# Folded maximum scans for five head pairs, with 64 more scans moved into the front part

## The chip, the cores and the metric

The kernel runs on one core of one Trainium2 chip. The metric is the device time of one execution in microseconds (us). Three runs of the kernel before gave 1754.66, 1750.93 and 1756.15 us; their median is 1754.66 us.

## The reference

Two mixers of the same input x (2048 rows of 512 numbers, fp32) are blended row by row by a gate:

```python
qkv = x @ wqkv                                  # 32 heads of 16 numbers
scores = einsum("bhqd,bhkd->bhqk", q, k) * Dh ** -0.5
a = softmax(scores) @ v, heads joined, @ wo     # attention
b = Cr @ (x @ Wr.T) - Ci @ (x @ Wi.T)           # real part of a 2-D Fourier transform
g = sigmoid((x * gate_w).sum(-1))
out = g * a + (1 - g) * b
```

The weights of the attention are scaled by 64, so the scores are large and the softmax needs the true maximum of every row of scores: exp(score - max) is what is summed.

## The kernel before, in words

TensorE (PE) does all products as fp32r matmuls with 512 columns. A product of full precision is made of three partial products, high times high, high times low and low times high; the low part is the rest that the high part leaves. A contraction of 128 rows is cut into two halves of 64 rows that run side by side in the array (`halves_of`, L141). Such a side-by-side pair is called a slot here.

**Scan.** The maximum of every row of scores is found first, in a pass of its own, the scan. Two heads make a pair, and there are 16 pairs (`NP`). For one pair, `scan(n, ps)` (L110) takes a block of 128 queries (`qb`, 16 of them) and a quarter of the keys (`c`, 4 quarters of 512). It issues two matmuls side by side, one for each head (L119), into a PSUM tile of two banks, and VectorE (DVE) reduces the tile to two maxima for each of the 128 queries with one `tensor_reduce` (L121). So a pair has 64 scans (`SCANS`), and all pairs have 1024 (`TOTAL`). After the 64th, `shift(p)` (L123) takes the maximum over the four quarters, transposes, splits and stores it in DRAM (`m_d`); the attention later reads it as two more rows of the query operand, so that its scores arrive in PSUM with the maximum subtracted.

**Front part (L150 to L504).** Here PE makes the projections of x to q and k (`project_t`, L280), to values and to the hidden Fourier transform (`project_s`, L303), and then the Fourier transform along the sequence (L455 to L502). q and k go to DRAM as high and low part (`q_d`, `k_d`); `row_loads` (L76) brings back the rows of one pair, and in the front part these loads are issued on ScalarE's (ACT) queue (`load_scan_beside`, L175). `products` (L201) and the Fourier loop call `beside()` (L183) after every slot. It runs the helpers that are due (`after`, `run_due`), and once `PACE` (3.9) slots have passed it puts one scan into PE's order. A scan's PSUM tile is one of two (`s1`, L155), used in turn; the projections use the two others (`xy`). The front part issues the first `FRONT` (564) scans. Order on every engine is the order in which the code issues; nothing is reordered.

**Attention part (L506 to L780).** 512 steps, 32 for each pair: 2 halves of the queries (`h`) by 16 blocks of keys (`kb`). A step computes scores with `qk2` (L532) for two query chunks: chunk 0 into one tile of two banks that exists once (tag `s3`, `bank2`), chunk 1 into two single banks out of three (tag `s2`, `bank`). ACT takes the exponential of chunk 0 in one instruction (L547) and of chunk 1 in two (L551). `pv` (L556) multiplies the exponentials with the values; its 16 PE instructions per two steps accumulate into `pvb`. While scans are left (`next_scan`, L728), each step also holds one scan between the two `qk2` calls, and each step runs the `pv` of the step before.

From step `MIX` on (L38, 512 less the steps without a scan, so step 461) there are no scans. Then a generator, `outputs()` (L693), mixes the finished heads with wo: `next(fill)` (L755, L765) yields a few slots per step. `mix_heads(t, steps)` (L653) makes 9 slots for row block t, spread as `steps` says, and `take_in` (L644) adds the gated result to the Fourier part `ys[t]` on DVE. From `MIX` on the `pv` work is grouped: none in an odd step, that of two steps in an even one (L769). Before, `mix_heads` used 4 or 2 steps for a row block, in all 51 steps. The Fourier part is read back from `y_d` for the row blocks 0 to 7 eleven steps ahead of `MIX` and for the others at step 480 (L751, `load_y`). What is left after the last step (L783 to L827) is a tail of some output blocks.

Of the kernel before, what the change touches and what calls it, by code (L numbers as in the profile page):

```python
# [34 lines left out]
FRONT = 564  # L35
PACE = 3.9
NWARM = 20
MIX = TOTAL - FRONT + 1  # L38
SLOW = 3


def build(tc, x, xT, wqkv, wo, wrT, wiT, cr, ci, gate, out):
    nc = tc.nc
    with ExitStack() as ctx:
# [6 lines left out]
        k_d = [dram.tile([P, 2, S], F32, name=f"k_d{f}") for f in range(ND)]  # L51
        m_d = [dram.tile([2, 4, 2, NB, 32], F32, name=f"m_d{p}") for p in range(NP)]
# [23 lines left out]
        def row_loads(p, queue):  # L76
# [4 lines left out]
            for j in range(2):  # L81
                b, r = 64 * j, slice(DH * ((2 * p + j) % 8), DH * ((2 * p + j) % 8) + DH)
                loads += [(ks[b:b + 32, :], k_d[p // 4][r, 0:1, :].to_broadcast([DH, 2, S])),
                          (qs[b:b + 32, :], q_d[p // 4][r, :, :].rearrange("e n s -> (e n) s")),
                          (ks[b + 32:b + 48, :], k_d[p // 4][r, 1, :]),
# [22 lines left out]
        mx = {}  # L108

        def scan(n, ps):  # L110

# [9 lines left out]
            nc.vector.tensor_reduce(mx[p][:, :, qb, c], ps, axis=AX.X, op=ALU.max)  # L121

        def shift(p):  # L123
# [10 lines left out]
            return [lambda: nc.vector.tensor_reduce(m, mx[p].rearrange("p j b c -> p (j b) c"), axis=AX.X, op=ALU.max,  # L134
                                                    negate=True),
# [12 lines left out]
        seen, slots, due = [0], [0], []  # L148
        pace = [None, 0.0]
        with ExitStack() as pf:  # L150
# [11 lines left out]
            def after(n, f, *args):  # L162

                due.append((slots[0] + n, len(due), f, args))
# [18 lines left out]
            def beside():  # L183
# [5 lines left out]
                pace[1] += 1.0 / pace[0]  # L189
# [60 lines left out]
            with ExitStack() as px:  # L250
# [28 lines left out]

                def project_t(w, dst, f, c, ps=None):  # L280
# [4 lines left out]
                    s = ep.tile([P, 512], F32, tag="ty", name="s")  # L285
# [9 lines left out]
                    def store(i, v):  # L295
                        nc.sync.dma_start(dst[f][:, i, c * 512:(c + 1) * 512], v.bitcast(F32))

                    after(9, nc.scalar.copy, hi, s)
# [62 lines left out]
                project_t(wk, k_d, 1, 0)  # L361
# [72 lines left out]
            with ExitStack() as py:  # L434
# [4 lines left out]

                for n in range(4, 8):  # L440
# [63 lines left out]
        assert seen[0] == FRONT  # L504

        with ExitStack() as pa:  # L506
# [347 lines left out]
```

## Time and profile before

| what | value |
|---|---|
| median of three runs | 1754.66 us (1750.93 to 1756.15) |
| profiled execution | 1756.16 us |
| its span, first to last instruction | 1754.4 us |
| PE busy | 1731.9 us, 99% of the span |
| DVE busy | 1347.4 us, 77% |
| ACT busy | 1166.8 us, 67% |
| POOL busy | 777.5 us, 44% |
| scans (L121) | 1024 of 1220 ns each by the mean, 1208.4 us |
| mean granted PE clock | 0.998 |

How to read it: matmuls are pipelined and their ends are modelled, so that PE is shown busy in nearly the whole span whatever bounds it. What bounds a stage is read from the pitch, the time from one start to the next, and from what an instruction waited for. The profile gives a share of each engine in 40 slices of 43.9 us. DVE is full in the slices 3 to 16 (the front part), ACT is full from slice 18 on (the attention part) up to the last three slices, which hold the steps without a scan.

### The profile page before, as it was taken

The page shows a single profiled execution, that of the slowest core. Times are in us where ns is not written, and L with a number is a line of the kernel's source. Part 1 is how long each engine was busy: PE and PEld are TensorE (multiplying, and loading weights), DVE is VectorE, ACT ScalarE, POOL GpSimd, SP SyncE. Part 2 cuts the span into 40 slices and gives each one's busy share as a digit, 9 for nine tenths or more (in the row PEclk, how much of TensorE's full clock was granted, in tenths as well). Part 3 has the DMA queues.
Part 4 walks back from the last instruction along what each step waited for, and adds up shares of the span by engine and source line. Part 5 has one row for each costly group of instructions (what it writes and reads, how often), then busy time and mean ns, then how long its engine had stood idle before and what let it go on. Part 6 is the DMA issues. An engine that isn't in the chain of part 4 may idle for free.

```text
span 1754.4 us, 33571 instructions
## 1 busy us (share of the span) xinstructions
PE 1731.9 (99%) x13640; PEld 988.3 (56%) x13640; DVE 1347.4 (77%) x1296; ACT 1166.8 (67%) x1894; POOL 777.5 (44%) x881
## 2 busy tenths in 40 slices
PE   8999999999999999999999999999999999999998
PEld 6987787878777787633333333333333333333554
DVE  6799999999999999866666666666666777765233
ACT  6445333000031000299999999999999999999885
POOL 3688557666677777413232322323232323323222
PEclk9999999999999999999999999999999999999999
DMA  7662455525474553633233351441433333453512
GB/s 263 224 199 74 128 156 177 138 92 133 129 188 134 136 150 112 145 61 62 58 63 61 57 99 25 87 72 42 79 66 61 65 67 72 85 108 91 138 41 100
DMA packets 119307, 185.79 MB, mean 106 GB/s; under 512 B 53184, under 2 KB 55728, under 8 KB 112240
## 3 DMA queue, kind: packets, MB, share of 16 engines
q1 hardware_dynamic: 77200, 148.96, 32.7%
q0 software_dynamic: 38496, 19.47, 5.3%
q10 hardware_dynamic: 3456, 15.21, 4.1%
q8 instruction: 107, 1.75, 0.5%
q14 instruction: 48, 0.39, 0.1%
HBM read 129.89 MB, written 53.22 MB: 104 GB/s over the span
## 4 chain that ended last, share of the span: by engine, by line
PE 80%; DVE 12%; DMA 3%; POOL 2%; issue 1%; ACT 1%; SPq 0%; DVEq 0%; ACTq 0%; POOLq 0%
PE pvb L558 27%; PE xy L145 21%; PE s L543 18%; PE s L119 11%; DVE mx L121 11%; PE s L145 3%; DMA lc<-ob 2%; POOL s L173 1%; POOL el L173 0%; DVE b L214 0%; DMA q_d<-eh 0%; DMA raws<-xT 0%; DMA raws<-wqkv 0%; POOL lc L566 0%; DVE y L645 0%
## 5 line engine op out<-in xcount | busy, mean ns | idle before, releaser
L121 DVE TENSOR_REDUCE mx<-s 128x2 f32<-128x1024 f32 x1024 | 1208.4, 1220 | 276.2 <-PE s L119 276.1
L551 ACT ACTIVATE e<-s 128x512 f32<-128x512 f32 x1024 | 630.4, 748 | 1.6 <-PE s L543 1.6
L547 ACT ACTIVATE eb<-s 128x1024 f32<-128x1024 f32 x512 | 600.2, 1172 | 23.0 <-PE s L543 23.0
L558 PE MATMUL pvb<-e,va 128*17 128x512 f32 x2048 | 528.5, 599 | 0.0
L558 PE MATMUL pvb<-eb,va 128*17 128x512 f32 x2048 | 528.3, 599 | 0.0
L543 PE MATMUL s<-qs,ks 50*128 50x512 f32 x2048 | 454.1, 442 | 0.0
L543 PEld LDWEIGHTS s<-qs,ks 50*128 50x128 f32 x2048 | 215.3, 184 | 418.4 <-ACT eb L547 389.5
L119 PE MATMUL s<-ks,qs 48*128 48x512 f32 x2048 | 418.7, 397 | 8.4 <-DVE mx L121 6.9
L496 ACT ACTIVATE tx<-xy,gm 128x512 f32<-128x512 f32 x32 | 22.1, 689 | 380.6 <-PE xy L145 329.7
L119 PEld LDWEIGHTS s<-ks,qs 48*128 48x128 f32 x2048 | 200.3, 184 | 45.5 <-DVE mx L121 20.0
L566 POOL DMA_DIRECT2D lc<-ob x124 | 63.1, 515 | 238.9 <-DVE ob L563 238.8
L558 PEld LDWEIGHTS pvb<-eb,va 128*17 128x17 f32 x2048 | 63.4, 95 | 174.9 <-issue 163.7
L573 POOL DMA_DIRECT2D r_d<-lc x31 | 18.1, 585 | 322.3 <-DVE lc L572 322.3
L145 PE MATMUL xy<-w,b 64*128 64x512 f32 x768 | 105.4, 392 | 0.2 <-ACT s L292 0.2
L645 DVE SCALAR_TENSOR_TENSOR y<-s,g,y 128x512 f32<-128x512 f32 x50 | 36.6, 748 | 81.5 <-PE s L145 80.9
L310 ACT ACTIVATE tx<-xy 128x512 f32<-128x512 f32 x48 | 28.7, 598 | 93.1 <-PE xy L145 91.5
L575 POOL DMA_DIRECT2D rb<-r_d x124 | 60.3, 493 | 54.0 <-DMA r_d<-lc 53.9
L145 PEld LDWEIGHTS xy<-w,b 64*128 64x128 f32 x768 | 72.9, 186 | 17.0 <-ACT s L292 0.7
L576 POOL TENSOR_TENSOR ob<-ob,rb 128x512 f32<-128x512 f32 x31 | 39.7, 1282 | 70.6 <-DMA rb<-r_d 68.8
L408 POOL TENSOR_TENSOR ab<-tx,ty 128x512 f32<-128x512 f32 x32 | 41.3, 1291 | 50.6 <-ACT ty L311 32.2
L558 PEld LDWEIGHTS pvb<-e,va 128*17 128x17 f32 x2048 | 63.3, 95 | 0.3 <-ACT e L551 0.3
L173 POOL TENSOR_TENSOR el<-s,eh 128x512 fp32r<-128x512 f32 x32 | 41.4, 1295 | 48.2 <-ACT eh L173 41.0
(928 smaller groups left out, 2085.8 us busy)
## 6 DMA issues: line engine op xcount, KB each, us to landing
craw<-ci SPq DMA_DIRECT2D x64, 256.0 KB
craw<-cr SPq DMA_DIRECT2D x60, 256.0 KB
ks<-k_d SPq DMA_DIRECT2D x48, 256.0 KB
qs<-q_d SPq DMA_DIRECT2D x48, 256.0 KB
ab_d<-ab SPq DMA_DIRECT2D x32, 256.0 KB
y_d<-y SPq DMA_DIRECT2D x32, 256.0 KB
o_d<-oh POOLq DMA_DIRECT2D x28, 256.0 KB, 9.8
o_d<-ol POOLq DMA_DIRECT2D x28, 256.0 KB, 15.3
```

The source lines that it names most:

```text
L119: nc.tensor.matmul(ps[:, j, :], qs[b:b + 48, qb * P:(qb + 1) * P], ks[b:b + 48, c * 512:(c + 1) * 512], start=True, stop=True)
L121: nc.vector.tensor_reduce(mx[p][:, :, qb, c], ps, axis=AX.X, op=ALU.max)
L145: nc.tensor.matmul(ps[j], lhs[r], rhs[r], start=first, stop=last)
L173: d[2](*d[3])
L408: nc.gpsimd.tensor_add(ab, tx, ty)
L543: nc.tensor.matmul(pss[j], ks[b:b + 50, kb * P:(kb + 1) * P], qs[b:b + 50, q0:q0 + 512], start=True, stop=True)
L547: nc.scalar.activation(e, ps, AF.Exp, scale=SCALE)
L551: nc.scalar.activation(e[j], pss[j], AF.Exp, scale=SCALE)
L558: nc.tensor.matmul(pvb[r:r + VC, :], va[:, kb, 2 * p + j, :], es[c][j], start=kb == 0, stop=kb == NB - 1, tile_position=(0, r))
L566: nc.gpsimd.dma_start(lc[32 * n:32 * n + 32, :], ob[r + DH:r + VC, :].rearrange("p (s e) -> p s e", e=16))
L575: nc.gpsimd.dma_start(rb[r:r + DH, :], r_d[p][h][n:n + 1, :].to_broadcast([DH, 512]))
L576: nc.gpsimd.tensor_mul(ob, ob, rb)
```

## The change

For the pairs 4 to 8 (`FOLDED`) the keys of the four quarters are combined two by two. With a and b the keys of two neighbouring quarters, max(q.a, q.b) = relu(q.(a - b)) + q.b for each pair of keys. `kf_d` holds a - b in the place of the even quarters and b in the place of the odd ones; it is built while the keys are projected (`fold_keys`). A scan of an even quarter then ends in ACT, which writes the positive part of the 128x1024 PSUM tile to SBUF (`fold`). A scan of an odd quarter ends in two `tensor_tensor_reduce` on DVE, one for each head, which add the PSUM half and the `fold` half and give the maximum. PE's scans stay as many as before, 64 for a pair. These five pairs' 320 scans are issued at a closer pace, and `FRONT` is 628 instead of 564. So the attention part holds 396 scans, `MIX` is step 397, and 115 steps have no scan; the 9 slots of a `mix_heads` are spread over 6 or 8 steps. For the row blocks 8 to 12 `mix_heads` starts before `load_y`, so it loads its own rows of `y_d`; the blocks 8 to 11 are also stored back there. While k is projected the pace is 4.2. In the order of the built program each `tensor_tensor_reduce` is two DVE instructions, the pass itself and one that writes 128x1.

```diff
-FRONT = 564
+FRONT = 628
 PACE = 3.9
+FOLDED = range(4, 9)
+FOLD_PACE = 3.15
+SLOW_PACE = 4.2
-SLOW = 3
...
-            nc.vector.tensor_reduce(mx[p][:, :, qb, c], ps, axis=AX.X, op=ALU.max)
+            if p not in FOLDED:
+                nc.vector.tensor_reduce(mx[p][:, :, qb, c], ps, axis=AX.X, op=ALU.max)
+            elif c % 2 == 0:
+                fold[0] = folds[0].tile([P, 2, 512], F32, tag="fold", name="fold")
+                nc.scalar.activation(fold[0], ps, AF.Relu)
+            else:
+                for j in range(2):
+                    nc.vector.tensor_tensor_reduce(out=fold[0][:, j, :], in0=ps[:, j, :], in1=fold[0][:, j, :],
+                                                   scale=1.0, scalar=-3.0e38, op0=ALU.add, op1=ALU.max,
+                                                   accum_out=mx[p][:, j, qb, c // 2:c // 2 + 1])
...
-                scanned[p], loads = row_loads(p, nc.scalar if p else nc.sync)
+                scanned[p], loads = row_loads(p, nc.scalar if p else nc.sync, kf_d if p in FOLDED else k_d)
...
-                pace[1] += 1.0 / pace[0]
+                pace[1] += (PACE / FOLD_PACE if seen[0] // SCANS in FOLDED else 1.0) / pace[0]
...
+                def fold_keys(f, c):
+
+                    a, b = half.pop(c - 1), half.pop(c)
+                    hi = ep.tile([P, 512], F32R, tag="eh", name="eh", bufs=3)
+                    lo = ep.tile([P, 512], F32R, tag="el", name="el")
+                    nc.gpsimd.tensor_sub(a, a, b)
+
+                    def store(i, v):
+                        nc.sync.dma_start(kf_d[f][:, i, (c - 1) * 512:c * 512], v.bitcast(F32))
+
+                    after(4, nc.scalar.copy, hi, a)
+                    after(5, nc.vector.tensor_sub, lo, a, hi.bitcast(F32))
+                    after(8, store, 0, hi)
+                    after(12, store, 1, lo)
...
-                for n, (f, c) in enumerate([(2, 0), (3, 0)] + [(f, c) for f in range(1, ND) for c in range(1, NC)]):
-                    if n == 2:
+                for n, (f, c) in enumerate([(f, c) for f in range(1, ND) for c in range(NC)]):
+                    if n == 0:
+                        scan_at(SLOW_PACE)
+                    if n == 3:
                         load_w(wv, wqkv[:, 1024:1536], 48, nc.gpsimd)
                     project_t(wk, k_d, f, c)
+                scan_at(PACE)
...
                 ps = pair_banks()
+                if t not in ys:
+                    y = ap.tile([P, D], F32, tag="take", name="yb", bufs=3)
+                    nc.sync.dma_start(y, y_d[t // 4][:, t % 4, :])
...
+                alone = t not in ys
+                if alone:
+                    ys[t] = y
                 for j in range(2):
                     take_in(t, ps[:, j, :])
+                if alone:
+                    nc.sync.dma_start(y_d[t // 4][:, t % 4, :], ys.pop(t))
...
-                        yield from mix_heads(t, (2, 2, 2, 3) if t < 2 * SLOW and t % 2 == 0 else (4, 5))
+                        yield from mix_heads(t, (1, 1, 1, 1, 1, 1, 1, 2) if t in (0, 5, 10) else (1, 2, 1, 2, 1, 2))
```

More of the change, by code (lines that the diff above doesn't have):

```diff
@@ L51, in build @@
         k_d = [dram.tile([P, 2, S], F32, name=f"k_d{f}") for f in range(ND)]
+        kf_d = [None] + [dram.tile([P, 2, S], F32, name=f"kf_d{f}") for f in range(1, ND)]
         m_d = [dram.tile([2, 4, 2, NB, 32], F32, name=f"m_d{p}") for p in range(NP)]
@@ L74, in build, with row_loads @@
         scanned, used = {}, {}
-        def row_loads(p, queue):
+        def row_loads(p, queue, keys=k_d):
             qs = stk.tile([P, S], F32R, tag="stk", name="qs")
@@ L296, in store @@
                         nc.sync.dma_start(dst[f][:, i, c * 512:(c + 1) * 512], v.bitcast(F32))
+                        if folded and c % 2:
+                            nc.sync.dma_start(kf_d[f][:, i, c * 512:(c + 1) * 512], v.bitcast(F32))
+                    if folded:
+                        half[c] = s
+                        if c % 2:
+                            after(11, fold_keys, f, c)
                     after(9, nc.scalar.copy, hi, s)
```

23 lines of the change are left out of this document (13 added, 10 removed).

## The prediction

> **What bounds the kernel now.** I read the page's busy times first, then the busy times of three stretches, then the chain that ended last, and then the timeline of a few microseconds in each stage.
>
> ```profile
> PE 1731.9 (99%) x13640; PEld 988.3 (56%) x13640; DVE 1347.4 (77%) x1296; ACT 1166.8 (67%) x1894; POOL 777.5 (44%) x881
> ```
>
> PE is shown busy everywhere, so the line decides nothing. The stretches do (columns: PE, PEld, DVE, ACT, POOL busy, with the number of instructions):
>
> ```profile
> 361.00:737.00 376.00, 372.69 (x3176) 297.30 (x3172) 369.69 (x341) 43.37 (x70) 255.61 (x251) 1.00 0.51 137
> 1493.00:1613.40 120.40, 119.48 (x884) 43.70 (x880) 81.63 (x77) 119.62 (x191) 35.62 (x55) 1.00 0.44 95
> 1613.40:1735.50 122.10, 122.10 (x992) 63.83 (x993) 36.66 (x53) 101.24 (x154) 26.17 (x39) 1.00 0.33 86
> ```
>
> The first stretch is the front part from the first scan of pair 4 (the first one to be folded) to its end. DVE is full (370 of 376 us) and ACT nearly idle (43), so DVE looks like the limit, and folding moves work from DVE to ACT. But PE is full too. The chain shows its pitch:
>
> ```profile
> 36.79 20.02 PE xy L145 x173
> 1631.31 1.84 PE pvb L558 x16
> 1635.68 1.84 PE pvb L558 x16
> 1640.73 1.84 PE pvb L558 x16
> 1728.16 1.84 PE pvb L558 x16
> 1733.20 1.84 PE pvb L558 x16
> ```
>
> 173 matmuls without scans take 20.02 us. Two run side by side, so a slot costs 20.02 / 86.5 = 0.2315 us. The stretch holds 3176 / 2 = 1588 slots, which are 367.6 of its 376 us. Only 8.4 us are not PE's own pitch. PE and DVE are balanced here: relieving DVE can return at most 8.4 us in this stretch, and each scan that is added costs PE a slot.
>
> The second stretch is the 63 steps before the first `mix_heads` step that the change takes scans from: 120.4 / 63 = 1.91 us each, with ACT full. The third is the steps without a scan: 122.1 / 51 = 2.39 us. ACT is not full there. Why, the timeline of two such steps says:
>
> ```profile
> 1628.71 0.73 PE L543 MATMUL s<-qs,ks 50*128 50x512 f32 x4
> 1629.25 1.02 ACT L547 ACTIVATE eb<-s 128x1024 f32<-128x1024 f32 x1 [0.50 <-PE s L543]
> 1629.28 1.10 PE L145 MATMUL s<-wo,oc 64*128 64x512 f32 x8
> 1630.33 0.29 PEld L543 LDWEIGHTS s<-qs,ks 50*128 50x128 f32 x3 [0.39 <-ACT eb L547]
> 1630.82 0.18 PEld L543 LDWEIGHTS s<-qs,ks 50*128 50x128 f32 x1 [0.19 <-ACT e L551]
> 1631.13 1.04 ACT L547 ACTIVATE eb<-s 128x1024 f32<-128x1024 f32 x1
> 1631.24 0.61 PE L558 MATMUL pvb<-eb,va 128*17 128x512 f32 x2
> 1633.08 0.73 PE L543 MATMUL s<-qs,ks 50*128 50x512 f32 x4
> ```
>
> At 1628.71 the odd step's scores start. The even step's scores wait for ACT to free the only `s3` tile (1630.33), then for an exponential to free a bank (1630.82). Then 16 instructions of `pv` run (1631.24 to 1633.08), and only then the next odd step's scores. That is a loop of 4.37 us per two steps: 1633.08 - 1628.71. The mixing slots are not in it; four of them (x8) fit into the wait, with 0.39 us to spare. The chain says the same: from 1631.31 to 1635.68 are 4.37 us. Where 9 slots fall on two steps it is 5.05 (1635.68 to 1640.73).
>
> **The change part by part.** The sum is made against the profiled execution: span 1754.4, time 1756.16 us, which is 1.5 above the median of the runs, 1754.66.
>
> **1. 64 more scans in the front part.** 64 x 0.2315 = +14.8 us on PE, which has no room there.
>
> **2. DVE's relief.** The waits of PE on DVE in this stretch are:
>
> ```profile
> PEld s L119 <- DVE mx L121: 9.3, 20, 1.2
> PE s L119 <- DVE mx L121: 2.7, 6, 0.7
> ```
>
> Weight loads run ahead, so their 9.3 us are not all lost. I take -3, near the matmuls' 2.7; bounds 0 and -8.4.
>
> **3. The folded keys.** Six times: one POOL subtraction, one ACT copy, one DVE subtraction, four stores on SP's queue. The nearest DVE row has the same form beside POOL:
>
> ```profile
> L214 DVE TENSOR_TENSOR b<-early,b 128x512 fp32r<-128x512 f32 x6 | 7.5, 1283 | 0.0
> ```
>
> 6 x 1.28 = 7.7 us of DVE, in a stage where DVE is the tighter of the two. The pace of 4.2 in its 144 slots takes 144/3.9 - 144/4.2 = 2.6 scans out of it, about 3 us of DVE. The DVE subtraction also waits for a low-part buffer that a store frees, and scans queue behind it. I take +2; bounds 0 and +8.
>
> **4. The folded scans.** A fold pass does not stand in the trace. Its cost is bounded by these rows:
>
> ```profile
> L121 DVE TENSOR_REDUCE mx<-s 128x2 f32<-128x1024 f32 x1024 | 1208.4, 1220 | 276.2 <-PE s L119 276.1
> 1745.93 3.37 DVE L645 SCALAR_TENSOR_TENSOR y<-s,g,y 128x512 f32<-128x512 f32 x5
> 1749.22 0.73 DVE L645 SCALAR_TENSOR_TENSOR y<-pvb,g,y 128x512 f32<-128x512 f32 x1
> 208.76 0.17 DVE L137 CAST chi<-mt 128x32 fp32r<-128x32 f32 x1
> 208.85 1.22 DVE L121 TENSOR_REDUCE mx<-s 128x2 f32<-128x1024 f32 x1
> L381 ACT ACTIVATION_READ_ACCUMULATOR xg<-xg 128x1 f32 x16 | 3.2, 202 | 0.0
> ```
>
> The nearest pass is L645: one operand in PSUM, one in SBUF, result in SBUF, 512 columns. Its pitch is (1749.22 - 1745.93) / 5 = 0.66 us. The second instruction of each pass, which writes 128x1, I put at a small DVE instruction's pitch, 208.85 - 208.76 = 0.09, with 0.17 until it is done; ACT's readout of 0.20 is the upper end. In the changed program's order the signal that frees the PSUM tile sits on the second readout. So a folded pair of scans holds DVE for D = 0.66 + 0.09 + 0.66 + 0.17 = 1.58 us, against 2 x 1.22 before. Bounds of D: 1.3 (two passes, readouts free) and 1.9.
>
> That fits into a pair's time on PE, 2 x (3.15 + 1) x 0.2315 = 1.92 us. But each scan keeps one of two PSUM tiles, in turn: all even ones go to the tile that ACT frees, all odd ones to the tile that DVE frees. So where two tiles used to cover one DVE pass, the odd scan now has one tile for itself, and PE's in-order queue stands until both passes of the last odd scan are done. Latencies, from the attention part:
>
> ```profile
> 900.26 0.40 PE L119 MATMUL s<-ks,qs 48*128 48x512 f32 x2
> 900.47 1.21 ACT L547 ACTIVATE eb<-s 128x1024 f32<-128x1024 f32 x1
> 900.71 1.23 DVE L121 TENSOR_REDUCE mx<-s 128x2 f32<-128x1024 f32 x1 [0.67 <-PE s L119]
> 902.35 1.22 ACT L547 ACTIVATE eb<-s 128x1024 f32<-128x1024 f32 x1
> ```
>
> Matmul to DVE: 900.71 - 900.26 = 0.45. Matmul to ACT: 1629.25 - 1628.71 = 0.54. An ACT pass of 128x1024 alone: 1.04; its end (1629.25 + 1.02 = 1630.27) to the engine that waits: 1630.33 - 1630.27 = 0.06. Let the even scan start at e, and PE wait x before the odd one, which starts at o = e + 0.96 + x. The fold pass starts at e + 0.54 + 1.04 + 0.06 = o + 0.68 - x, but not before o + 0.45. The next odd scan starts 1.58 + 0.06 after that, and this is 1.92 + x after o. So 0.68 - x + 1.64 = 1.92 + x: x = 0.20, a pair takes 2.12 us. (The start, o + 0.48, is just late enough.) Of 160 folded pairs about 5 lie in the stretch of pace 8 and wait for nothing: 155 x 0.20 = +31 us. With D = 1.3, x = 0.06 and +9; with D = 1.9 the floor of 0.45 holds, a pair takes 0.45 + 1.9 + 0.06 = 2.41, and it is +76.
>
> ACT's own work gets in the way too:
>
> ```profile
> L496 ACT ACTIVATE tx<-xy,gm 128x512 f32<-128x512 f32 x32 | 22.1, 689 | 380.6 <-PE xy L145 329.7
> ```
>
> `tx` and `ty` hold ACT for about 1.2 us once per 48 slots, so 21 times in 155 pairs; a positive part that falls behind them comes late by 1.2 x 1.2 / 2 / 2.1 = 0.35 on average: +7, bounds 0 and +15. Without the cover of two tiles this shows in full.
>
> At this place the Trainium skill speaks against the change: "Vector Engine (DVE) Microarchitecture Reference", section 7, says of the instruction form with two sources and an accumulator that two sources in SBUF that are not bf16 halve its rate. Here one source lies in PSUM, so by its letter the pass keeps its rate; no row before shows it. The sum by it, if PSUM counted, is the third rival.
>
> **5. The attention part.** Up to step 396 nothing changes. From 397 to the last step (1493.0 to 1735.5) are 242.5 us now. After, the mixing needs 1 to 3 slots in the wait of a pair of steps, but the loop of 4.37 us doesn't hold them, so fewer of them shorten nothing: 57 x 4.37 = 249.1. The last three pairs keep their 9 slots and 5.04 (1728.16 to 1733.20): +2.0. So 251.1, or +8.6. The 64 steps that lose their scan rise from 1.91 to 2.185, since the grouping of `pv` starts 64 steps earlier; that eats what the spreading saves. The extra `y_d` loads start six steps (13 us) before they are read and cost nothing; if SP's queue were blocked a `take_in` would come late: 0 to +4.
>
> **Sum:** 14.8 - 3 + 2 + 31 + 7 + 8.6 = 60.4. 1756.2 + 60.4 = 1816.6 in the profiled execution's terms, 1815 against the median.
>
> **The rivals.**
>
> *No wait at the odd tile* (pass and readout overlap, D at or under 1.3). Then terms 1, 2, 3 and 5 remain: 14.8 - 3 + 2 + 8.6 = 22, or 1777. For it: 0.06 of wait is little, and L645's pitch may be high for this pass. Against it: the readout is an instruction of its own. It is still slower, because PE's pitch in the front and the loop in the attention stay.
>
> *A dearer readout* that waits for its pass to drain (D = 1.9): 22 + 76 + 7 = +105, 1860.
>
> *A pass at half rate*, 1.32 instead of 0.66, because the maximum that it carries along costs it a second beat, or because POOL, busy 256 of 376 us here, holds SBUF against it as in the row of 1283 ns: D = 2 x (1.32 + 0.09) + 0.08 = 2.9, a pair takes 0.45 + 2.9 + 0.06 = 3.41, +231; 22 + 231 + 7 makes 2016. Against it: L645 has the same places of operands, and all of its 50 took the same beside POOL:
>
> ```profile
> L645 DVE SCALAR_TENSOR_TENSOR y<-s,g,y x50: 735/751/752, 1621.2 to 1748.6; 128x512 f32<-128x512 f32 x50
> ```
>
> The rule of the Trainium skill's page above would be this rival's first cause.
>
> *Faster:* the steps without a scan fall to ACT's own pitch, 902.35 - 900.47 = 1.88 us, and the odd tile never waits. 114 x 1.88 = 214 against 242.5 is -28; with 14.8 - 8.4 it makes -22, or 1733. It decides at `pv`: it needs the next scores to start before the 16 `pv` instructions end. Against it: with 4 slots or with 5 the pair of steps took 4.37, and PE's order there is the same in both programs.
>
> **How the numbers follow.** The wait at the odd tile (forecast, 1815, own range 1790 to 1840) 0.59; no wait (1777) 0.20; dearer readout 0.08; half rate 0.05; faster 0.05; gains and losses that cancel 0.03. The likeliest says 1815. The range of 8 in 10 takes in the forecast, the case without a wait and its bounds, down to 1772, and part of a dearer readout, up to 1850. A measurement of this kernel can tell about 0.3% (5 us) from no change. Faster by more 0.05, within 0.03, slower by more 0.92.
>
> **What would show it.** The first exponential of the attention part starts near 737 + 52 = 789 us (terms 1 to 4 and ACT's 7); near 751 there is no wait. In the folded stretch the scan matmuls pair up at 2.12 us, and the waits list PE's scan matmuls behind the fold line's DVE instructions with some 30 us. Fold passes show a pitch of 0.66 and a readout of 0.09. DVE's share falls there, and PE's idle time rises. From step 397 on two `pv` groups stand 4.37 us apart. If they stand 3.76 apart, or if the front ends before 745, the prediction is wrong.

## The result, and the profile after

The changed kernel takes 1836.76 us, the median of four runs (1833.01 to 1839.99), beside 1754.84 for the kernel before in the same series. The ratio is 1.047, with a 95% interval of 1.0442 to 1.0498: **slower by 4.7%**, in the direction that was forecast, and 22 us above the forecast of 1815. The profiled execution took 1839.99 us; its span is 1838.2. Line numbers are those of the changed kernel from here on, unless another kernel is named.

From the page of the changed kernel, the busy times and the two new groups:

```profile
PE 1777.5 (97%) x13640; PEld 979.1 (53%) x13640; DVE 1194.4 (65%) x1622; ACT 1332.4 (72%) x2060; POOL 784.0 (43%) x887
L135 DVE CUSTOM_DVE_ANT_0 fold<-s,fold 128x512 f32<-128x512 f32 x320 | 208.2, 688 | 112.4 <-ACT fold L132 76.7
L132 ACT ACTIVATE fold<-s 128x1024 f32<-128x1024 f32 x160 | 164.4, 1027 | 146.0 <-PE s L126 135.9
```

DVE lost 153 us of work and ACT got 166. The change did what it says, and that says nothing of the time. To see where 84 us went, I cut both traces at four events: the first matmul of scan 256 (the first folded scan), and the exponentials (the L591 group, L547 in the kernel before, one for each step) that begin step 0, step 397 and step 511.

| stage | before, us | after, us | difference | forecast |
|---|---|---|---|---|
| start to scan 256 | 360.2 | 390.9 | +30.7 | +2 |
| scan 256 to step 0 | 376.5 | 409.4 | +32.9 | +49.8 |
| step 0 to step 397 | 756.2 | 759.9 | +3.6 | 0 |
| step 397 to step 511 | 242.5 | 259.2 | +16.7 | +8.6 |
| the rest | 18.9 | 18.8 | -0.1 | 0 |

The forecast's sum is 60.4 us and the measured one 83.8. It is short by 23 us because one term is far too small, one too large and one half of what it should be. Busy times of stretches of the changed kernel (columns as in the prediction; the granted PE clock, the DMA share and GB/s stand last):

```profile
56.40:160.80 104.40, 85.51 (x650) 67.95 (x649) 80.26 (x70) 41.14 (x78) 68.32 (x54) 0.90 0.60 204
390.90:800.30 409.40, 405.38 (x3291) 300.43 (x3289) 290.83 (x731) 202.46 (x229) 254.71 (x251) 1.00 0.46 129
1741.60:1756.20 14.60, 8.39 (x51) 3.14 (x52) 2.10 (x3) 6.04 (x11) 2.03 (x4) 0.77 0.47 173
```

The first row holds the first 64 scans: the end of q's projections, those of k, and the first ones of the values. The same 64 scans in the kernel before:

```profile
56.60:131.40 74.80, 73.97 (x632) 69.09 (x632) 73.19 (x64) 35.43 (x68) 58.09 (x46) 1.00 0.60 195
```

104.4 us against 74.8: 29.6 of the first +30.7 arise here, long before any scan is folded. PE and DVE are both idle for about a fifth of the stretch; nothing is full. Whatever holds them is a wait. Five of the changed kernel's waits between 50 and 260 us (total, times, longest):

```profile
ACT eh L190 <- POOL s L190: 31.2, 15, 6.2
PEld s L126 <- DVE mx L129: 24.0, 14, 5.3
PE s L126 <- DVE mx L129: 19.1, 8, 4.9
DVE el L190 <- ACT eh L190: 14.1, 5, 4.5
POOL el L190 <- DMA kf_d<-el: 13.2, 3, 5.2
```

In the kernel before, the only wait for a reduction in this window is a small one:

```profile
PEld s L119 <- DVE mx L121: 2.7, 8, 0.6
```

The five are a chain over four engines, read from below: POOL waits for a store to free a low-part buffer, ACT's cast waits for POOL, DVE's subtraction waits for ACT's cast, and PE's scan waits for the reduction that stands behind the subtraction in DVE's order. DVE's timeline has the six folded subtractions:

```profile
84.17 1.11 DVE L190 TENSOR_TENSOR el<-s,eh 128x512 fp32r<-128x512 f32 x1 [1.74 <-ACT eh L190]
96.40 1.08 DVE L190 TENSOR_TENSOR el<-s,eh 128x512 fp32r<-128x512 f32 x1 [4.33 <-ACT eh L190]
106.38 1.10 DVE L190 TENSOR_TENSOR el<-s,eh 128x512 fp32r<-128x512 f32 x1 [0.63 <-ACT eh L190]
117.61 1.09 DVE L190 TENSOR_TENSOR el<-s,eh 128x512 fp32r<-128x512 f32 x1 [4.46 <-ACT eh L190]
129.80 1.09 DVE L190 TENSOR_TENSOR el<-s,eh 128x512 fp32r<-128x512 f32 x1 [2.94 <-DMA k_d<-eh]
141.80 1.09 DVE L190 TENSOR_TENSOR el<-s,eh 128x512 fp32r<-128x512 f32 x1 [2.92 <-ACT eh L190]
```

The brackets, in which DVE stood idle with reductions queued behind, sum to 17.0 us; the six subtractions take 6.6. POOL's timeline ahead of the second of them shows the other end:

```profile
89.94 1.29 POOL L190 TENSOR_TENSOR el<-s,eh 128x512 fp32r<-128x512 f32 x1 [5.21 <-DMA kf_d<-el]
91.20 1.29 POOL L190 TENSOR_TENSOR s<-s,tx 128x512 f32<-128x512 f32 x1
93.22 1.27 POOL L190 TENSOR_TENSOR el<-s,eh 128x512 fp32r<-128x512 f32 x1 [0.73 <-ACT eh L190]
94.44 1.27 POOL L304 TENSOR_TENSOR s<-s 128x512 f32<-128x512 f32 x1
```

POOL stands 5.21 us for a buffer, does the projection's own three instructions and only then the difference a - b (L304), which DVE has been waiting for.

The folded stretch itself, one pair and a half of it, from the timeline of the changed kernel:

```profile
479.68 0.69 DVE L135 CUSTOM_DVE_ANT_0 fold<-s,fold 128x512 f32<-128x512 f32 x1 [1.09 <-ACT fold L132]
480.29 1.03 ACT L132 ACTIVATE fold<-s 128x1024 f32<-128x1024 f32 x1 [0.64 <-PE s L126]
480.29 0.08 DVE L135 DVE_READ_ACCUMULATOR2_ANT mx<- 128x1 f32 x1
480.29 0.69 DVE L135 CUSTOM_DVE_ANT_0 fold<-s,fold 128x512 f32<-128x512 f32 x1
480.91 0.08 DVE L135 DVE_READ_ACCUMULATOR2_ANT mx<- 128x1 f32 x1
481.04 0.50 PE L126 MATMUL s<-ks,qs 48*128 48x512 f32 x2
481.69 0.69 DVE L135 CUSTOM_DVE_ANT_0 fold<-s,fold 128x512 f32<-128x512 f32 x1 [0.70 <-PE s L126]
482.07 0.40 PE L126 MATMUL s<-ks,qs 48*128 48x512 f32 x2
483.06 0.51 PE L126 MATMUL s<-ks,qs 48*128 48x512 f32 x2
```

Odd scans start at 481.04 and 483.06: 2.02 us a pair. The odd scan at 481.04 starts 0.05 after the last readout ends (480.91 + 0.08), its pass 0.65 after it, and the two passes with their readouts hold DVE for 1.31 (479.68 to 480.99): 0.65 + 1.31 + 0.05 is the loop. It is the odd tile's loop that the prediction described, but what binds this pair is the time from the odd scan to its pass, which the prediction had as a floor, and not the end of ACT's pass: ACT's at 480.29 ends at 481.32, and the pass that needs it starts at 481.69.

At step 481 there is a stall that the kernel before doesn't have. Some rows of the changed kernel's PE there:

```profile
1743.03 0.60 PE L602 MATMUL pvb<-eb,va 128*17 128x512 f32 x2
1743.57 0.73 PE L587 MATMUL s<-qs,ks 50*128 50x512 f32 x4
1750.51 1.65 PE L161 MATMUL s<-wo,oc 64*128 64x512 f32 x6 [6.21 <-DVE y L689]
1752.94 1.04 PE L602 MATMUL pvb<-eb,va 128*17 128x512 f32 x2
1753.77 1.06 PE L602 MATMUL pvb<-eb,va 128*17 128x512 f32 x2
1755.11 0.60 PE L602 MATMUL pvb<-eb,va 128*17 128x512 f32 x2
```

PE waits 6.21 us for the addition of row block 12, and two steps of 8.52 and 3.56 us stand where 1.88 and 2.49 are usual: 7.7 us lost.

### The profile page after: what moved, and what is told of

It reads as the page before. It is cut to its first block, busy times and chain, and to the rows that moved or that the text cites. A ratio compares the mean times of both kernels' runs of the same rounds, so it can differ in the third digit from the quotient of the medians.

```text
span 1838.2 us, 34450 instructions
## 1 busy us (share of the span) xinstructions
PE 1777.5 (97%) x13640; PEld 979.1 (53%) x13640; DVE 1194.4 (65%) x1622; ACT 1332.4 (72%) x2060; POOL 784.0 (43%) x887
## 3 DMA queue, kind: packets, MB, share of 16 engines
q8 instruction: 107, 1.75, 0.4%
## 4 chain that ended last, share of the span: by engine, by line
PE 48%; ACT 6%; DVE 5%; DMA 2%; issue 1%; POOL 0%; SPq 0%; DVEq 0%; POOLq 0%
PE pvb L602 24%; PE s L587 16%; PE s L126 5%; ACT eb L591 5%; DVE mx L129 4%; PE xy L161 2%; DMA lc<-ob 2%; ACT e L595 2%; PE s L161 1%; DMA or<-o_d 0%; DVE y L689 0%; POOL lc L610 0%; DVE fold L135 0%; DVE ob L607 0%; SPq L679 0%
## 5 line engine op out<-in xcount | busy, mean ns | idle before, releaser
L129 DVE TENSOR_REDUCE mx<-s 128x2 f32<-128x1024 f32 x704 | 838.3, 1220 | 245.2 <-PE s L126 245.1
L595 ACT ACTIVATE e<-s 128x512 f32<-128x512 f32 x1024 | 616.7, 721 | 1.9 <-PE s L587 1.9
L591 ACT ACTIVATE eb<-s 128x1024 f32<-128x1024 f32 x512 | 586.1, 1145 | 41.4 <-PE s L587 41.4
L126 PE MATMUL s<-ks,qs 48*128 48x512 f32 x2048 | 431.9, 411 | 28.1 <-DVE mx L129 25.6
L135 DVE CUSTOM_DVE_ANT_0 fold<-s,fold 128x512 f32<-128x512 f32 x320 | 208.2, 688 | 112.4 <-ACT fold L132 76.7
L132 ACT ACTIVATE fold<-s 128x1024 f32<-128x1024 f32 x160 | 164.4, 1027 | 146.0 <-PE s L126 135.9
L689 DVE SCALAR_TENSOR_TENSOR y<-s,g,y 128x512 f32<-128x512 f32 x42 | 30.6, 748 | 136.8 <-PE s L161 116.5
L190 ACT CAST eh<-s 128x512 fp32r<-128x512 f32 x38 | 23.6, 620 | 61.2 <-POOL s L190 31.2
```

The lines of the kernel that those rows point to most:

```text
L126: nc.tensor.matmul(ps[:, j, :], qs[b:b + 48, qb * P:(qb + 1) * P], ks[b:b + 48, c * 512:(c + 1) * 512], start=True, stop=True)
L132: nc.scalar.activation(fold[0], ps, AF.Relu)
L135: nc.vector.tensor_tensor_reduce(out=fold[0][:, j, :], in0=ps[:, j, :], in1=fold[0][:, j, :], scale=1.0, scalar=-3.0e38, op0=ALU.add, op1= ...
L190: d[2](*d[3])
L591: nc.scalar.activation(e, ps, AF.Exp, scale=SCALE)
L595: nc.scalar.activation(e[j], pss[j], AF.Exp, scale=SCALE)
```

## The experiments

Twelve kernels ran. The times are medians, with the ratio to the kernel before on the same chip and its 95% interval; the other columns are from each kernel's trace. The kernel before and the changed one stand first. Beside the twelve, the kernel before had medians of 1754.2 to 1756.0 us, so medians of different series compare to within some 2 us.

| kernel | us | ratio (interval) | scan 256 at | step 0 at | steps 397 to 511 |
|---|---|---|---|---|---|
| before | 1754.8 | | 360.2 | 736.7 | 242.5 |
| changed | 1836.8 | 1.047 (1.0442 to 1.0498) | 390.9 | 800.3 | 259.2 |
| e1 no folded keys | 1808.0 | 1.0312 (1.029 to 1.0335) | 365.0 | 774.1 | 257.9 |
| e2 low part on POOL | 1832.4 | 1.0442 (1.0425 to 1.0459) | 387.1 | 796.5 | 259.1 |
| e3 no ring buffers | 1828.4 | 1.0416 (1.039 to 1.0443) | 376.6 | 785.5 | 258.4 |
| e4 sums loaded earlier | 1830.8 | 1.0435 (1.0418 to 1.0451) | 389.9 | 799.1 | 253.6 |
| e5 folded, pace 3.9 | 1781.5 | 1.0155 (1.0139 to 1.0171) | 390.2 | 762.4 | 241.5 |
| e6 folded, pace 3.15 | 1796.6 | 1.0241 (1.0225 to 1.0257) | 389.4 | 775.8 | 241.5 |
| e7 p v ungrouped | 1829.7 | 1.0431 (1.0414 to 1.0449) | 387.9 | 797.1 | 253.1 |
| e8 own buffers, later | 1821.9 | 1.0383 (1.0366 to 1.04) | 375.9 | 785.6 | 258.4 |
| e9 ungrouped, slots late | 1824.0 | 1.0389 (1.0374 to 1.0403) | 389.9 | 799.2 | 246.0 |
| e10 before, ungrouped | 1766.1 | 1.006 (1.0046 to 1.0073) | 359.0 | 735.4 | 253.4 |
| e11 four edits | 1810.2 | 1.0312 (1.0297 to 1.0327) | 378.6 | 787.9 | 242.1 |
| e12 e2 and e3 together | 1828.3 | 1.0412 (1.0394 to 1.0429) | 383.2 | 793.1 | 259.4 |

### What the folded keys cost: e1, e2, e3, e8, e12

My theory was that the first 30 us are DVE's order: a reduction stands behind a subtraction that waits for another engine. The first run leaves the making of the folded keys out.

```diff
-                scanned[p], loads = row_loads(p, nc.scalar if p else nc.sync, kf_d if p in FOLDED else k_d)
+                scanned[p], loads = row_loads(p, nc.scalar if p else nc.sync, k_d)
...
-                    s = rp.tile([P, 512], F32, tag="raw", name="s") if folded else ep.tile([P, 512], F32, tag="ty", name="s")
+                    s = ep.tile([P, 512], F32, tag="ty", name="s")
...
-                        if folded and c % 2:
-                            nc.sync.dma_start(kf_d[f][:, i, c * 512:(c + 1) * 512], v.bitcast(F32))
...
-                    if folded:
-                        half[c] = s
-                        if c % 2:
-                            after(11, fold_keys, f, c)
```

> The changed kernel without the folded keys: no differences of key quarters are made, split or stored, no right quarters are stored a second time, and the folded scans read the plain keys (so the maxima are not those of the reference). Theory (the making of the folded keys holds the scans up): the first folded scan, which began at 390.9 us in the changed kernel and at 361.0 us in the kernel before, begins near 363, the rest is as it was, and the time falls by some 27 us to about 1810. Rival (what holds the front up is the new order of the projections and the lower pace of 4.2 there, or DMA of the scans' operands): the first folded scan stays above 382 and the time above 1828.

Scan 256 began at 365.0, the time was 1808.0. The theory's numbers hold: making and storing the folded keys costs 25.9 of the 30.7 us. The other 4.8 came with the new order of the projections and the pace of 4.2; I didn't part these two. PE's waits for reductions between 50 and 260 us fall from 43 us to 5, in e1:

```profile
PEld s L126 <- DVE mx L129: 3.7, 9, 1.3
PE s L126 <- DVE mx L129: 1.2, 2, 0.9
```

From scan 256 to step 0 this kernel takes 409.1, as the changed one does (409.4): the keys cost nothing later.

Then the chain itself. Take the subtraction off DVE:

```diff
-                    after(5, nc.vector.tensor_sub, lo, a, hi.bitcast(F32))
+                    after(5, nc.gpsimd.tensor_sub, lo, a, hi.bitcast(F32))
```

> One word changed: the low part of a folded key quarter is taken off by GpSimd in place of VectorE, which then no longer stands in its order behind ScalarE's cast of it. Work added to GpSimd: 12 instructions of some 1.3 us. Theory (VectorE's order: a scan's maximum stands behind a subtraction that waits 4.4 us for the cast): the first folded scan begins 15 to 25 us earlier than 390.9, near 370, and TensorE's waits for a maximum in 50 to 260 us fall from 43 us to below 20. Rival A (the cast itself, in ScalarE's order behind GpSimd, holds ScalarE's copies out of PSUM and through them TensorE): the waits move from VectorE to ScalarE and the first folded scan stays above 383. Rival B (GpSimd, the fuller now, becomes later for every projection): above 391.

387.1, and 1832.4: the theory's 370 failed, and rival A came true. (Six subtractions move to POOL, not the twelve that the expectation counts.) PE hardly waits for reductions now, but for ACT's copies out of PSUM, in e2:

```profile
PEld xy L161 <- ACT s L327: 15.9, 7, 3.7
PE xy L161 <- ACT s L327: 12.8, 7, 3.2
PEld s L126 <- DVE mx L129: 3.7, 9, 1.3
```

The cast that waits for POOL stands in ACT's order just as the subtraction stood in DVE's, and ahead of the copies that free the projections' PSUM. Cutting the last link of the chain only moves the wait to the link before. The next run cuts the first one, POOL's wait for a buffer:

```diff
-                    hi = ep.tile([P, 512], F32R, tag="eh", name="eh", bufs=3)
-                    lo = ep.tile([P, 512], F32R, tag="el", name="el")
+                    hi, lo = b.bitcast(F32R), a.bitcast(F32R)
```

> The two parts of a folded key quarter are written over its own two sources, so that the fold takes no buffer of the projections' rings for high and low parts (the sources' ring of 3 is held longer instead). Theory (the length of the stand is the wait of GpSimd's low part for a buffer that a store to DRAM frees, 13.2 us in three places, and what stands behind it): GpSimd's waits for the store of a folded low part are gone, VectorE's stands in front of the fold's subtraction fall from 4.4 us to 2 or less, and the first folded scan begins near 375. Rival (the stand is GpSimd's own queue, not the buffers): stands stay at 4 us and the first folded scan within 4 us of 390.9. Third: the ring of 3 sources binds instead, and it begins later than 391.

Scan 256 began at 376.6 and the median was 1828.4. The profiled execution, of 1821.7 us, was the shortest of its four (up to 1831.3), so that the median's gain of 8 us is the safer number than the trace's 14. DVE's stands fell only by half, not to 2 us or less each, in e3:

```profile
DVE s L190 <- ACT s L190: 8.8, 4, 2.8
```

So buffers are half of it. The fourth run takes other buffers and also puts cast and subtraction later in the order:

```diff
-                    lo = ep.tile([P, 512], F32R, tag="el", name="el")
-                    nc.gpsimd.tensor_sub(a, a, b)
+                    lo = b.bitcast(F32R)
+                    nc.gpsimd.tensor_sub(b, a, b)
...
-                    after(4, nc.scalar.copy, hi, a)
-                    after(5, nc.vector.tensor_sub, lo, a, hi.bitcast(F32))
-                    after(8, store, 0, hi)
-                    after(12, store, 1, lo)
+                    after(8, nc.scalar.copy, hi, b)
+                    after(11, nc.vector.tensor_sub, lo, b, hi.bitcast(F32))
+                    after(12, store, 0, hi)
+                    after(15, store, 1, lo)
```

> The folded key's difference is taken into its second source and its low part over it, so that no buffer of the low parts' ring is used, and ScalarE's cast and VectorE's subtraction are due 8 and 11 slots after the difference in place of 4 and 5. Theory (VectorE and ScalarE stand because their parts are put in their order before GpSimd can have done its own, 1.3 us each for the projection's low part and the difference): the stands in front of the fold's subtraction are below 1 us each and the first folded scan, 390.9 us in the changed kernel and 376.6 with the buffers alone changed, begins at 364 to 370; the time is near 1813. Rival (what is left after the buffers is the work itself and the stores of a second set of keys): it begins at 374 or later, the time is 1822 or more.

375.9 and 1821.9: the rival's numbers, at their very edge. The volume of the stores is not what is left: e8 makes all the stores of the changed kernel and moves 232 GB/s in its first 64 scans (its row stands in the last section), where the changed kernel moves 204. The trace lets me count the rest. In e8:

```profile
DVE s L190 <- ACT eh L190: 5.1, 3, 2.0
```

The first 64 scans take 78.4 us without folded keys (e1). They take 86.9 in e8, which is 8.5 more; its stands are 5.1 and its six subtractions 6.2 us, 11.3 together. In e3 it is 12.9 more, with 8.8 and 7.1, 15.9 together. In the changed kernel it is 26.0 more, with 17.0 and 6.6, 23.6 together. Stands and work on DVE, less some 3 us that the lower pace leaves free, give the cost in the first two. In the changed kernel there are some 5 us beyond that; the last section comes back to them.

The last run of this group asks whether DVE's work was the rest, by putting e2 and e3 together.

> The two edits of the folded keys together: their parts written over their sources, and the low part taken off by GpSimd. With the folded keys left out the first folded scan began at 365.0 us, with the parts written over the sources alone at 376.6: 11.6 us are unexplained. Theory A (they are VectorE's six subtractions of 1.1 us and what stands behind them): it begins at 368 to 371 and the time is near 1822. Theory B (they are ScalarE's casts standing behind GpSimd, which holds its copies out of PSUM, as it was with the low part on GpSimd alone): it begins at 375 or later, and TensorE's waits for a copy out of PSUM on ScalarE exceed 15 us in 50 to 260 us.

383.2, and 1828.3, the same median as e3. Theory B: PE again waits for ACT's copies, 24.8 us in all, in e12:

```profile
PEld xy L161 <- ACT s L326: 13.7, 6, 3.4
PE xy L161 <- ACT s L326: 11.1, 6, 2.9
```

What follows: the price of the folded keys is, for the most part, a chain POOL, ACT, DVE through queues that keep their order, placed in 4 and 5 slots (about 1 us) after a POOL instruction that lasts 1.3 us and stands behind others. No variant that I ran makes the keys for less than about 14 us above e1 by the medians. None leaves out what nobody reads, either: `fold_keys` runs six times, twice for each of three groups of four pairs (4 to 7, 8 to 11, 12 to 15), but `FOLDED` ends at pair 8, so the keys of the last group are made and stored for no scan. What these two of the six cost is not measured.

### The wait at the odd tile: e5 and e6

Theory: the fold costs PE nothing but a wait where a pair's pitch is below the loop of 2.02 to 2.08 us. Two kernels with the same instructions and two paces tell it apart from a price of the fold itself. Both fold the pairs 4 to 7 only, and have the 564 front scans and the attention part of before.

```diff
-FRONT = 628
+FRONT = 564
-FOLDED = range(4, 9)
+FOLDED = range(4, 8)
-FOLD_PACE = 3.15
+FOLD_PACE = 3.9
...
-                        yield from mix_heads(t, (1, 1, 1, 1, 1, 1, 1, 2) if t in (0, 5, 10) else (1, 2, 1, 2, 1, 2))
+                        yield from mix_heads(t, (2, 2, 2, 3) if t < 6 and t % 2 == 0 else (4, 5))
```

That is e5; e6 leaves `FOLD_PACE` at 3.15.

> Folding kept for pairs 4 to 7, but the scans stand at the old pace of 3.9 and 564 of them in the front part, as in the kernel before; the attention part is that of before too. A folded pair of scans then has 2.32 us of TensorE's work between its two starts (two slots pitches of 1.16 us, from 74.4 us for 64 scans in the kernel before), more than the 2.08 that the fold took in the changed kernel. Theory (the price of folding is a wait at the odd tile, which shows only where the pair's pitch is below the 2.08 us of relu, tile and two passes): no waits there, waits for the line of the passes below 8 us, the front ends some 28 us after that of before (the keys' price alone), near 766, and the time is near 1783. Rival (the fold costs something at any pace): the time is 1800 or more.

> The same with the pace of 3.15 for the folded scans, so the same instructions with 1.96 us of TensorE's work in a folded pair. Theory: the wait at the odd tile is back, 0.12 to 0.16 us for each of 128 pairs, and the time is 15 to 20 us above the kernel at pace 3.9. Rival (the pace is without effect, as all the work is the same and TensorE sets the end): within 4 us of it.

1781.5 against an expected 1783, and e6 is 15.1 us above it, against an expected 15 to 20. The theory holds. PE's wait for the folded passes between 360 and 800 us, in e6 and then in e5:

```profile
PEld s L126 <- DVE mx L135: 32.4, 90, 0.9
```

```profile
PEld s L126 <- DVE mx L135: 3.0, 10, 0.8
```

These are waits of weight loads, which lie beside the matmuls: they differ by 29.4 us where the times differ by 15.1, so such a row is not the price.

e5 also gives the price of folding without the wait. From scan 256 to step 0 it takes 372.2 us, against 376.5 in the kernel before: DVE's relief is worth 4.3 us, and that is all that folding brings here. Its scan 256 begins 30.0 us later than before, for the keys and the new order; less the 4.3 this is nearly all of the 27 us by which it is slower.

### The steps without a scan: e4, e7, e9, e10, e11

The stall at step 481 first. Row block 12 needs its sum `y` there, and `load_y` for the blocks 12 to 15 is issued at step 480.

```diff
-                if step in (MIX - 11, (NP - 1) * PERIODS):
-                    for c in range(2):
-                        load_y(c + 2 * (step > MIX))
+                for c, at in enumerate((MIX - 11, MIX - 11, (NP - 1) * PERIODS, (NP - 1) * PERIODS - 10)):
+                    if step == at:
+                        load_y(c)
```

> The last four row blocks' sums so far are loaded 10 steps earlier (step 470 for 480). Theory (the stall of 7.7 us at steps 481 and 482 is row block 12's addition on VectorE waiting 19.8 us for a load that is issued in the same step): the stall goes, steps 397 to 511 take 251 to 252 us in place of 259.2, and the time falls by 7 to 8 us to about 1829. Rival (the stall is the release of PSUM for p v by the copy of the last pair's sums, and the addition only waits beside it): the time stays within 2 us of the changed kernel's.

253.6, and 1830.8: 5.6 of the 7.7 us are gone, so the load was the cause, not the release of PSUM. The two steps are 4.01 and 2.49 now; 2.1 us remain, since the load was not let out at step 470 either. SP's waits in e4:

```profile
SPq L684 <- PE s L587: 21.3, 1, 21.3
```

SP had to wait for a buffer that the scores of pair 14 were still reading.

Then the pitch of 4.38 us for two steps. The prediction put it to the grouping of `pv`. If so, ungrouping it must bring some 30 us:

```diff
-                for _ in range(min(len(pend), 1) if step < MIX else 0 if step % 2 else 2):
+                for _ in range(min(len(pend), 1)):
...
-            flush()
-            flush()
+            while pend:
+                flush()
```

> The changed kernel with one p v in every step of the last 115 in place of two in every second. Theory (the scan-free steps last 4.38 us by twos because the even step, 2.50 us, holds two p v of 0.92 us and one or two thirds of a row block beside the products, while the odd step stays at ScalarE's 1.88): every step is 1.88 to 2.0 us, steps 397 to 511 take 218 to 228 us in place of 259.2, and the time is near 1803. Rival (TensorE's work of the two steps together is the bound, or the switching between products and p v, which grouping halves): steps 397 to 511 take 250 us or more.

253.1 of steps 397 to 511, 1829.7: 6 to 7 us. Two steps are 1.88 and 2.34 now, 4.22 together. The theory falls: grouping costs only 0.08 us a step here. PE is full by the rival, but its order could also be the reason: in e7 the longer step has a part of a row block on PE right before the first product. Moving it behind the second one:

```diff
-                if step >= MIX and step % 2 == 0:
-                    next(fill)
                 es = [qk2(p, h, kb, 0)]
...
-                if step >= MIX and step % 2:
+                if step >= MIX:
                     next(fill)
```

> The ungrouped kernel (one p v in every step), and every part of a row block is put behind the step's second product, where before the even steps had theirs in front of the first. Theory A (order: in the longer step, 2.34 us of the ungrouped kernel, the first product of the next step stands on TensorE behind p v and a part of a row block, and ScalarE waits for it): the longer step falls to 2.0 us or less, steps 397 to 511 take 228 to 240 us in place of 253.1, the time is near 1813. Theory B (TensorE is full: with 100.0 us busy of 100 in 1590 to 1690 its work of two steps, some 4.2 us, is the bound whatever its order): steps 397 to 511 stay within 4 us of 253.1.

246.0, between A (228 to 240) and B (249 and more). Most steps with one slot are at ACT's 1.88 now; steps with two, and the first step of a row block, mostly take 2.08 to 2.14. So the order was worth 7 us. What remains I put to PE's work in the fuller steps; no run shows it. Neither theory had the number.

The kernel before has more slots in its steps, nine in two steps for most row blocks. Does ungrouping help there too?

> The kernel before with one p v in every step of its last 51 in place of two in every second. Theory A (grouping makes the even step long): 51 steps gain some 0.15 to 0.3 us each, 7 to 15 us, near 1743. Theory B (TensorE is full there): within 4 us of the kernel before, since the ungrouped changed kernel gained 0.08 us a step (4.22 us for two in place of 4.38): 51 of these are 4 us at most.

Slower by 10 us (1.006, interval 1.0046 to 1.0073), which neither theory had. With 9 slots in two steps these take 5.61 us ungrouped and 5.04 grouped. ACT's and PE's timelines in e10 (L543 scores, L145 slots of row blocks, L558 `pv`, L547 exponential):

```profile
1663.04 1.05 ACT L547 ACTIVATE eb<-s 128x1024 f32<-128x1024 f32 x1
1666.80 1.03 ACT L547 ACTIVATE eb<-s 128x1024 f32<-128x1024 f32 x1 [1.73 <-PE s L543]
```

```profile
1662.82 1.36 PE L145 MATMUL s<-wo,oc 64*128 64x512 f32 x8
1664.11 0.61 PE L558 MATMUL pvb<-eb,va 128*17 128x512 f32 x2
1665.09 1.43 PE L145 MATMUL s<-wo,oc 64*128 64x512 f32 x10
1666.36 0.63 PE L543 MATMUL s<-qs,ks 50*128 50x512 f32 x4
```

All nine slots and a `pv` stand on PE in front of one first product (1662.82 to 1666.36), and ACT idles 1.73 us. Grouped, four of the slots lay in PE's wait for ACT, as the prediction says. Grouping is a cover for slots: worth 10 us with nine of them, and costing 7 with three.

Last, four edits together (e3, e4, e7, e9), to see whether the gains add up.

> Four edits together: the folded keys' parts written over their sources, the last four row blocks' sums loaded at step 470, p v ungrouped, and all parts of row blocks behind the second product. If they add up: the measured gains of 8.3, 6.0 and 7.1 us, and what the last is worth by itself, come off 1836.8, which is 1815 with nothing for the last and about 1795 with 20 for it. If the first and the others share a cover: above 1822. In any case above the kernel before, 1754: the folded scans' waits and the 64 more scans stay.

1810.2. The measured single gains are 8.3, 6.0 and 7.1 us, and 5.7 from e7 to e9; 1836.8 less these is 1809.7. They add up. The stall is not wholly gone: the steps 481 and 482 still take 5.80 and 3.21 us. The time is still 3.1% above the kernel before, and none of the runs beats that kernel.

## Why the prediction was right and where it failed

**The sign** was right, for its reasons: in the stretch of the folded scans PE and DVE were balanced, so that DVE's relief returned 4.3 us (e5; forecast 3), while the front part got 64 more scans, and nothing came back in the attention part, where a scan had been hidden behind ACT. It does not hang on the term that failed: without the folded keys (e1) the kernel is still 3.1% slower. That the time lies within the forecast's own range (1790 to 1840) is partly luck: what was 29 us too little up to scan 256 and 8 too little in the steps without a scan met 17 us too much in the folded stretch.

**Step 3, the folded keys, is the one that failed:** +2 with bounds 0 and +8, and it was +30.7 (25.9 for the keys by e1, 4.8 for order and pace). The prediction priced DVE's own 7.7 us of work and set about 3 us against it for the scans that the lower pace takes out; how +2 comes from these it does not say. It named the wait for a buffer and the scans queued behind it, but gave them no size of their own; the upper bound was the work alone. The runs showed 17.0 us of stands besides 6.6 of work, on a queue with the scans' reductions behind.

**Step 4, the wait at the odd tile,** had the right mechanism and came out too large: +31 and +7 for ACT, against 15.1 us for 128 pairs between e5 and e6, so 18.9 for 160. A pair takes 2.07 on average (the 147 pairs below 2.5 us; the others stand at other paces) and not 2.12. Two sizes were off in opposite directions. The readout does not follow a pass but lies beside the next one (both start at 480.29), so D is 1.31, at the lower bound of 1.3 and not 1.58. And the pass starts 0.65 us after its scan, 0.54 at the least, where the row of a reduction had given 0.45; with D = 1.31 the prediction's formula would have made it 1.98. So mostly the floor binds, 0.65 + 1.31 + 0.05, where the prediction had ACT's pass as the binding term: in half of the pairs the pass starts 0.13 us or more after ACT's pass has ended, and 0.03 would be enough. In e5, at the wider pace, the time from scan to pass is 0.55; where the other 0.1 comes from stays open. The rivals with a dearer readout and with half the rate fell with this.

**Steps 1 and 2:** no run isolates the 14.8 us for 64 scans. The changed kernel's step 0 is 24.5 us after that of e6, which lacks the 64 scans and pair 8's folding. Of these 1.5 lie ahead of scan 256. 14.8 for slots and 32 pairs' waits, at 0.118 us (15.1 / 128) to 0.147 (2.067 less 1.92), make 18.6 to 19.5; 3.5 to 4.4 us stay unexplained.

**Step 5, the attention part:** 4.38 for two steps where 4.37 was forecast, with three slots in them in place of four or five, so the +8.6 was right for all but one place. Of the other 8.1 us, 7.7 are the stall at step 481. The prediction looked at the new loads of `y_d` (0 to +4), and not at the old load at step 480, which spreading the row blocks had moved from ahead of its reader to right at it. The reason given for 4.37, that the next scores stand behind the grouped `pv`, was only partly right: `pv` in every step and a later place for the slots (e7 and e9) together take 13 us out of the stage, half by each.

**Steps 0 to 396:** +3.6 in the profiled execution. The same code took 755.2 to 759.6 us in the twelve runs, so this is scatter.

**The rule of the Trainium skill** that spoke against the change ("Vector Engine (DVE) Microarchitecture Reference", section 7: two sources in SBUF that are not bf16 halve the rate of a form with two sources and an accumulator) keeps its limit here: with one source in PSUM a pass starts 0.61 us after the one before, 1.2 ns for each of its 512 columns, as the plain reduction has with 1220 ns for 1024. There is no halving, and POOL's work beside it changed nothing: 320 passes took 675 to 692 ns. The trace names the pass CUSTOM_DVE_ANT_0; whether that is the form of the rule, no run shows.

```profile
L135 DVE CUSTOM_DVE_ANT_0 fold<-s,fold x320: 675/687/692, 392.6 to 738.3; 128x512 f32<-128x512 f32 x160
```

## What to carry to other kernels

An instruction put into an engine's order costs its stand on top of its length (17.0 us and 6.6 here): before adding one, follow its inputs back through every queue and every ring of buffers, and put it where the slowest of them is done. Taking the last link of such a chain off the engine that stands only moves the stand (e2, e12); buffers and later places shorten it (e3, e8). Relieving an engine that is 98% busy gains little where another is 99% busy (4.3 of 376 us here), and a load that was early becomes late when the work that reads it is spread out.

## What the runs showed of the hardware that I had not expected

**A stand can cost more than its length, because TensorE's granted clock falls.** In the PE rows at step 481 above, the same `pv` matmuls take 0.60 us before the stand of 6.21 us, 1.04 to 1.06 after it, and 0.60 again from 1755.11 on, 4.6 us after PE set in. The granted clock of that stretch is 0.77, and 0.90 in the first 64 scans of the changed kernel, where PE's waits for a reduction last up to 4.9 us. It is 0.98 in e8, whose stands are short (up to 2.0 us on DVE), and 1.00 in e1, which has none of them; the first 64 scans of e8 and then of e1:

```profile
56.00:142.90 86.90, 79.62 (x652) 67.19 (x651) 78.69 (x70) 40.10 (x75) 66.31 (x52) 0.98 0.69 232
56.60:135.00 78.40, 76.61 (x650) 64.95 (x649) 74.12 (x64) 37.63 (x72) 60.27 (x48) 1.00 0.58 192
```

The same 650 matmuls keep PE busy for 85.51 us in the changed kernel and for 76.61 in e1 (ends are modelled). The difference of 8.9 us is large enough for the 5 us that the changed kernel lost beyond DVE's stands and work, and I put them here; no run isolates them. The Trainium skill, "TensorE: Matmul & The Clock Gate", "What's actually happening", says that an idle window of about 3.4 us halves the clock until PE has been busy for as long. The trace agrees in kind: after a stand of 6.21 us the durations are 1.05 / 0.60 = 1.75 times as long, not quite twice (their ends are modelled, so this is no reading of the clock itself), and they are back after 4.6 us.

**The accumulator's readout is nearly free.** It takes 83 ns and overlaps the next pass, but for the last one of a pair, on which the release of the PSUM tile waits.
